# Last row pair of the first MLP product: P5 with hi and lo weights in one tile, its upper half copied after the hi part, the gelu table loaded earlier, one operand job later

## The chip, the cores and the metric

The kernel runs on one core of one Trainium2 chip. The metric is the device time of one execution in microseconds (us). A core has a matrix engine (TensorE, PE in the profile, with its weight loads as PEld), VectorE (DVE), ScalarE (ACT), GpSimd (POOL), which here does little more than issue the transfers that add to memory, and SyncE (SP), which issues the plain transfers.

## The reference

The input x has 2048 tokens of 640 channels. With xn the layer norm of x, the result is

```python
return x + _A_ref(xn, ...) + _B_ref(xn, B_w1, B_b1, B_w2, B_b2)
# A: a = xn @ hid_re.T, b = xn @ hid_im.T ; y = seq_re @ a - seq_im @ b   (real part of a 2D DFT)
# B: h = layernorm(xn); u = gelu(h.T @ w1 + b1); y = (u @ w2 + b2).T      (MLP across the tokens)
```

w1 is 2048 x 1728 and w2 1728 x 2048. 1728 is 13 blocks of 128 and a rest of 64, the "tail".

## The kernel before, in words

**Precision.** Every operand in float32 is split in two: a "hi" part, rounded to the matrix engine's fast float format by a ScalarE copy (`high`, L138), and a "lo" part, the rest, by a VectorE subtraction (`low`, L141). A product is three matmuls (`three`, L149, L150, L152): hi weights by hi data, hi weights by lo data, lo weights by hi data. When the lo weights are None, the third is left out.

**Seven products.** All big products are done in 2 x 2 blocks with seven products P1 to P7 in place of eight (a Strassen-like scheme). A unit is one pair of output row blocks, and its seven steps run in the order P1, P5, P6, P2, P7, P3, P4 (`row_steps`). The four output blocks C11, C12, C21, C22 are (row, half) = (0,0), (0,1), (1,0), (1,1); a half is 320 of the 640 channels. Sums of the weight blocks are made on VectorE: `first_sum` (L785) makes s = A21 + A22, others (L144) follow. A step's products run over 4 (or 5) blocks of 128 in the contraction, so 12 (or 15) matmuls of 320 columns.

**Stages.** First the sequence DFT (matmuls of 512 columns, until 405 us), then the hidden DFT (8 units, "hid"), then the first MLP product in two halves of the contraction (`up`, stage 0 and 1, 7 units each), then the second MLP product (`down`, twice 8 units). In `up`, unit r makes the row blocks r and r + 7 of the 1728 rows. Stage 0 stores its result to DRAM (`part_up[r]`, L907); stage 1 fetches that and adds it (L911, a POOL transfer), applies the gelu on ScalarE (L916), and so on.

**The last unit, r = 6, is special** (`tail`): its second row block has only 64 real rows. For P7 and P4, which use that block alone, the weight tile of 128 columns holds the hi part in the first 64 and the lo part in the other 64 (`cut_piece` with tail), so that two matmuls do the work of three, 8 per step instead of 12. The upper 64 rows of such a result are the lo weights' share. They are copied by ScalarE into a buffer (`by_dram`, L945), and a POOL transfer adds them to `part_up[6]` in DRAM (`add_to`, L934, 64 x 320). In stage 0 these adds are kept in the list `halves` and issued behind the store of the unit (`end`). In stage 1 the buffers of `by_dram` serve in every unit, for P2 and P7 (L941, 128 x 320): they are four quarters of one buffer, chosen by r and the product. P7 of unit 0 takes the quarter that P7 of the tail unit of stage 0 had.

**Where P5's result goes before.** P5 and P3 share a bank: P5's read copies it to C22, P3 then accumulates on top, and P3's read adds both to C12. P6 accumulates on P1's bank; P6's read copies to C12 and, in the tail unit, adds to C22 (L858, VectorE) and copies to C21 (L859, ScalarE).

**Order of the work.** Nothing is scheduled by a program; the order is written by hand (`turn_of`). Turn i issues, on the in-order queues: the loads of that turn, the read of the result of step i - 1, the sums, the hi part for step i + 2, the `extras`, the `timed` ones, a job, the lo part for step i + 2, and the matmuls of step i. So whatever waits on ScalarE or VectorE in a turn holds up the hi or lo part behind it. A "job" prepares the moving operand of a later stage. Long jobs (the tuples) only run in the turns that `LONG_AT` allows, as a pattern (positions, period) for each stage; the first pair is for hid. Another turn takes a job only if the next one is short.

Of the kernel before, what the change touches and what calls it, by code (L numbers as in the profile page):

```python
# [11 lines left out]
AF = mybir.ActivationFunctionType  # L12
ALU = mybir.AluOpType

P = 128
# [6 lines left out]
TAIL = F - NF * P  # L22
# [39 lines left out]


LONG_AT = (
    ((0, 1, 3, 6), 7), ((0, 1, 3, 6, 7, 8, 10, 14, 15, 17, 20), 21), ((0, 1, 3, 6), 7), ((0, 1, 3), 7),
)


# [1 line left out]
def fnet_plus_mixer(  # L70
# [99 lines left out]
    def cut_piece(source, n, tail=False, stacked=False):  # L170

        held = {}

        def of_tail():
            hi, src = (t.rearrange("p (q c) -> p q c", c=P) for t in (held["piece"][:, 0, :n], source()))
            return hi[:, :, :TAIL], hi[:, :, P - TAIL :], src[:, :, :TAIL]

        def top():  # L180
            cut_turn[0] = (cut_turn[0] + 1) % (AHEAD + 1)
            held["piece"] = keep.tile([P, 2, D], R32, name="piece", tag=f"cut{cut_turn[0]}")
            if tail:
                hi, _, src = of_tail()
                high(hi, src)
            else:
                high(held["piece"][:, 0, :n], source())

        def bottom():
            if tail:  # L190
                hi, lo, src = of_tail()
                low(lo, src, hi)
                return held["piece"][:, 0, :n], None
            hi, lo = (held["piece"][:, i, :n] for i in range(2))
            if stacked:
                last = slice(n - P, n)
                low(hi[TAIL:, last], source()[TAIL:, last], hi[TAIL:, last])
            whole = n - P if stacked else n
            low(lo[:, :whole], source()[:, :whole], hi[:, :whole])
            return hi, lo  # L200

        return top, bottom
# [564 lines left out]
    def row_steps(stage, nq, load_piece, at, end, bias=(None, None), base=None, earliest=0, each=None, aside={}, tail=False, stacked=()):  # L767

        s0, n = len(steps), nq * P
        raw, banks, held = {}, {}, {}

        def load(*names):
            for name in names:
                raw[name] = raw_slot(n)
                load_piece(raw[name], int(name[1]) - 1, int(name[2]) - 1)  # L780

        def first_sum():
            k = n if n == D else CH
            raw["s"] = raws[k][:, raws[k].shape[1] - 1, :n]
            nc.vector.tensor_add(raw["s"], raw["A21"], raw["A22"])  # L785
            if stacked:

                at = slice(n - P, n)
                nc.vector.tensor_copy(raw["s"][TAIL:, at], raw["A21"][TAIL:, at])

        order = (1, 5, 6, 2, 7, 3, 4)

        early = n < D
        loads_of = {-6: ("A11", "A21", "A22"), -4: ("A12",)} if early else {
            -5: ("A11",), -4: ("A21", "A22"), -1: ("A12",),
        }
        operand = {1: "A11", 5: "s", 6: "A11", 2: "A12", 7: "A21", 3: "A12", 4: "A22"}

        sums_of = {
            -2: (first_sum, lambda: sub(raw["A21"], raw["A11"], raw["A21"])),  # L800
            -1: (lambda: sub(raw["A11"], raw["s"], raw["A11"]),),
            2: (lambda: sub(raw["A12"], raw["A12"], raw["A11"]),),
        }
        bank_of = {1: "z", 6: "z", 7: "z", 4: "z", 5: "y", 3: "y", 2: "w"}
        new_bank = (1, 5, 2)
        if tail:
            bank_of.update({7: "v", 4: "v"})
            new_bank += (7,)
        of_moving = {1: 0, 2: 1, 3: 2, 5: 3, 7: 4, 4: 5, 6: 6}

        goes_to = {1: (0, 0, True), 5: (1, 1, True), 6: (0, 1, True), 2: (0, 0, False), 7: (1, 1, False),
                   3: (0, 1, False), 4: (1, 0, True)}

        def products(i):
            def run(w):
                if i in new_bank:
                    banks[bank_of[i]] = bank()
                for q in range(nq):
                    ks = slice(q * P, (q + 1) * P)
                    m = moving[stage, q]  # L820
                    three(
                        banks[bank_of[i]][:, :H2],
                        (w[0][:, ks], None if w[1] is None or i in stacked and q == nq - 1 else w[1][:, ks]),
                        (m[:, 0, of_moving[i], :], m[:, 1, of_moving[i], :]), i in new_bank and q == 0, q == nq - 1,
                    )
            return run

        def read(i):
            def run():
                if i == 1:  # L830
                    held["c"] = place[at]()
                row, half, fresh = goes_to[i]
                cols = slice(half * H2, (half + 1) * H2)
                c, b = held["c"][:, row, cols], banks[bank_of[i]][:, :H2]
                if tail and i in (7, 4):
                    nc.vector.tensor_add(c[:TAIL], b[:TAIL], c[:TAIL])
                    aside[i](row, half, b)
                elif i in aside:
                    aside[i](row, half, b)
                elif not fresh:  # L840
                    nc.vector.tensor_add(c, b, c)
                elif base and i == 4:

                    for k, queue in enumerate((nc.sync, nc.scalar)):
                        of = slice(k * H2 // 2, (k + 1) * H2 // 2)
                        nc.vector.tensor_add(c[:, of], b[:, of], base()[:, row, cols][:, of])
                        each(c, row, half, True, of, queue)
                    return
                elif base:
                    nc.vector.tensor_add(c, b, base()[:, row, cols])  # L850
                elif bias[row] is not None:
                    nc.scalar.activation(c, b, AF.Identity, bias=bias[row])  # L852
                else:
                    nc.scalar.activation(c, b, AF.Copy)  # L854
                if tail and i == 6:

                    low_row = held["c"][:, 1, :]
                    nc.vector.tensor_add(low_row[:, H2:], b, low_row[:, H2:])  # L858
                    nc.scalar.activation(low_row[:, :H2], b, AF.Copy)  # L859
                if each:  # L860
                    each(c, row, half, i in (2, 7, 3, 4))
                elif i == 4:
                    end(held["c"])
            return run

        for e, names in loads_of.items():
            loads[max(s0 + e, earliest)].append(lambda names=names: load(*names))
        if s0 == s_hid:


            operand[6] = "s"
            behind_lo[s0 - 2].append(first_sum)
            sums_of = {
                0: (lambda: sub(raw["s"], raw["s"], raw["A11"]),),
                1: (lambda: sub(raw["A21"], raw["A11"], raw["A21"]),),
                2: (lambda: sub(raw["A12"], raw["A12"], raw["s"]),),
            }
        for e, fs in sums_of.items():
            sums[s0 + e].extend(fs)
        for e, i in enumerate(order):  # L880
            steps.append(cut_piece(lambda i=i: raw[operand[i]], n, tail and i in (7, 4), i in stacked) + (products(i),))
            reads[s0 + e + 1].append(read(i))
        return s0

# [13 lines left out]
    def up(stage, r, at):  # L898
# [34 lines left out]
        def add_to(t, rows, row, half):  # L933
            nc.gpsimd.dma_start(part_up[r][rows, row, half * H2 : (half + 1) * H2], t, accum_op=ALU.add)  # L934

        def by_dram(i):
            def run(row, half, b):

                t = place["x1"]()[:, (r + (i == 4)) % 2, i // 7 * H2 : (i // 7 + 1) * H2]
                if not (tail and i in (7, 4)):  # L940
                    nc.scalar.activation(t, b, AF.Copy)  # L941
                    add_to(t, slice(P), row, half)
                    return
                t = t[P - TAIL :]
                nc.scalar.activation(t, b[P - TAIL :], AF.Copy)  # L945
                if stage == 0:
                    halves.append((row, half, t))
                else:
                    add_to(t, slice(TAIL), row, half)
            return run  # L950

        aside = (2, 7) if stage else ()
        if tail:
            aside += (7, 4)
        s0 = row_steps(
            f"up{stage}", 4, load_piece, at, end, earliest=s_up - 4, aside={i: by_dram(i) for i in aside}, tail=tail,
        )
# [65 lines left out]
    for r in range(NF2):  # L1023
# [4 lines left out]
        [gets[1]] + rests[0] + [gets[2]] + changes[1] + rests[1] + [gets[3]] + changes[2] + rests[2]  # L1028
        + changes[3] + rests[3]
    ))  # L1030
    for r in range(NF2):
        up(1, r, ("x2", "ca", "cb", "v", "x0")[r % 5])
    s_down = len(steps)
# [99 lines left out]
```

## Time and profile before

| | us |
|---|---|
| median of 3 runs (lowest, highest) | 876.68 (876.0, 876.92) |
| the profiled execution, whole | 875.92 |
| its span (first to last instruction) | 874.2 |
| mean granted TensorE clock | 0.999 |
| TensorE busy | 869.0 (99%) |
| VectorE / ScalarE / GpSimd busy | 711.7 / 530.2 / 126.2 |

A row of a timeline has the start, the duration, the engine, the line, the operation and what it writes and reads; in brackets stands how long the engine had been idle before it, and what ended that. [...] In a list of transfers the last number is the time from issue to landing. Times in a timeline count from the start of the span.

### The profile page before, as it was taken

The page shows a single profiled execution, that of the slowest core. Times are in us where ns is not written, and L with a number is a line of the kernel's source. Part 1 is how long each engine was busy: PE and PEld are TensorE (multiplying, and loading weights), DVE is VectorE, ACT ScalarE, POOL GpSimd, SP SyncE. Part 2 cuts the span into 40 slices and gives each one's busy share as a digit, 9 for nine tenths or more (in the row PEclk, how much of TensorE's full clock was granted, in tenths as well). Part 3 has the DMA queues.
Part 4 walks back from the last instruction along what each step waited for, and adds up shares of the span by engine and source line. Part 5 has one row for each costly group of instructions (what it writes and reads, how often), then busy time and mean ns, then how long its engine had stood idle before and what let it go on. Part 6 is the DMA issues. An engine that isn't in the chain of part 4 may idle for free.

```text
span 874.2 us, 13999 instructions
## 1 busy us (share of the span) xinstructions
PE 869.0 (99%) x4924; PEld 793.1 (91%) x4924; DVE 711.7 (81%) x1217; ACT 530.2 (61%) x960; POOL 126.2 (14%) x170
## 2 busy tenths in 40 slices
PE   9999999999999999999999999999999999999998
PEld 6888888888888888889999999999999999999998
DVE  7878878795887978788887787998678978897887
ACT  5746576764556566557565556675577766555553
POOL 0110100101121111222010101000212221111211
PEclk9999999999999999999999999999999999999999
DMA  7771554619385556869666756454678797766786
GB/s 270 231 266 76 194 203 132 242 59 357 54 219 92 163 119 133 208 92 195 168 127 166 156 139 196 162 177 138 142 170 181 169 244 193 190 136 133 151 173 139
DMA packets 86087, 147.64 MB, mean 169 GB/s; under 512 B 8512, under 2 KB 35904, under 8 KB 85760
## 3 DMA queue, kind: packets, MB, share of 16 engines
q1 hardware_dynamic: 64928, 95.80, 34.0%
q0 software_dynamic: 20800, 50.70, 30.6%
q8 instruction: 38, 0.62, 0.3%
q14 instruction: 33, 0.27, 0.1%
q10 hardware_dynamic: 288, 0.25, 0.1%
HBM read 99.96 MB, written 52.00 MB: 174 GB/s over the span
## 4 chain that ended last, share of the span: by engine, by line
PE 94%; DVE 3%; ACT 1%; DMA 1%; issue 1%; DVEq 0%; ACTq 0%
PE psum L149 30%; PE psum L150 30%; PE psum L152 29%; PE psum L477 5%; DVE piece L141 1%; DMA pieces<-y 1%; DVE pieces L144 0%; DMA x<-in_x 0%; ACT piece L138 0%; ACT n L259 0%; ACT x L259 0%; DVE pair L144 0%; DVE st L210 0%; DVE pieces L785 0%; DVE shid L141 0%
## 5 line engine op out<-in xcount | busy, mean ns | idle before, releaser
L141 DVE TENSOR_TENSOR piece<-pieces,piece 128x512 fp32r<-128x512 f32 (+2 forms) x524 | 350.1, 671 | 125.8 <-ACT piece L138 119.1
L138 ACT ACTIVATE piece<-pieces 128x512 fp32r<-128x512 f32 (+3 forms) x508 | 318.1, 627 | 212.0 <-PE psum L152 143.5
L150 PE MATMUL psum<-piece,n 128*128 128x512 f32 x504 | 196.4, 390 | 0.0
L149 PE MATMUL psum<-piece,n 128*128 128x512 f32 x504 | 196.2, 389 | 0.0
L152 PE MATMUL psum<-piece,n 128*128 128x512 f32 x504 | 196.1, 389 | 0.0
L149 PE MATMUL psum<-sup,piece 128*128 128x320 f32 x392 | 121.2, 310 | 0.0
L149 PE MATMUL psum<-sdown,piece 128*128 128x320 f32 x392 | 121.0, 309 | 0.0
L150 PE MATMUL psum<-sup,piece 128*128 128x320 f32 x392 | 120.9, 309 | 0.0
L150 PE MATMUL psum<-sdown,piece 128*128 128x320 f32 x392 | 120.9, 309 | 0.0
L152 PE MATMUL psum<-sup,piece 128*128 128x320 f32 x376 | 116.6, 310 | 0.0
L152 PE MATMUL psum<-sdown,piece 128*128 128x320 f32 x376 | 116.2, 309 | 0.0
L144 DVE TENSOR_TENSOR pieces<-pieces 128x512 f32<-128x512 f32 (+3 forms) x142 | 112.7, 794 | 2.6
L150 PEld LDWEIGHTS psum<-piece,n 128*128 128x128 f32 x504 | 94.6, 188 | 21.0 <-DVE piece L141 1.5
L149 PEld LDWEIGHTS psum<-piece,n 128*128 128x128 f32 x504 | 94.6, 188 | 19.9
L152 PEld LDWEIGHTS psum<-piece,n 128*128 128x128 f32 x504 | 94.6, 188 | 19.3
L152 PE MATMUL psum<-shid,piece 128*128 128x320 f32 x280 | 86.6, 309 | 0.1
L150 PE MATMUL psum<-shid,piece 128*128 128x320 f32 x280 | 86.5, 309 | 0.0
L149 PE MATMUL psum<-shid,piece 128*128 128x320 f32 x280 | 86.5, 309 | 0.0
L854 ACT ACTIVATE pair<-psum 128x320 f32<-128x320 f32 x102 | 44.5, 436 | 54.6 <-PE psum L152 49.8
L149 PEld LDWEIGHTS psum<-sup,piece 128*128 128x128 f32 x392 | 73.6, 188 | 0.6 <-ACT pairs L854 0.3
L149 PEld LDWEIGHTS psum<-sdown,piece 128*128 128x128 f32 x392 | 73.6, 188 | 0.2 <-ACT pair L852 0.2
L150 PEld LDWEIGHTS psum<-sup,piece 128*128 128x128 f32 x392 | 73.6, 188 | 0.0
(106 smaller groups left out, 1115.8 us busy)
## 6 DMA issues: line engine op xcount, KB each, us to landing
pieces<-in_dft_seq SPq DMA_DIRECT2D x128, 256.0 KB, 5.4
pieces<-in_w SPq DMA_DIRECT2D x88, 256.0 KB, 3.7
y<-c POOLq DMA_DIRECT2D x84, 256.0 KB, 6.1
out<-pair POOLq DMA_DIRECT2D x38, 320.0 KB, 5.3
pieces<-y SPq DMA_DIRECT2D x32, 320.0 KB, 3.9
pieces<-in_w SPq DMA_DIRECT2D x32, 192.0 KB, 3.1
out<-in_x SPq DMA_DIRECT2D x16, 320.0 KB, 7.1
up<-pair POOLq DMA_DIRECT2D x8, 640.0 KB, 3.2
```

Source lines behind the costliest of these rows:

```text
L138: nc.scalar.activation(hi, src, AF.Copy)
L141: nc.vector.tensor_sub(lo, src, hi.bitcast(F32))
L144: nc.vector.tensor_sub(to, a, b)
L149: nc.tensor.matmul(psum, wh, mh, start=first, stop=False, skip_group_check=True)
L150: nc.tensor.matmul(psum, wh, ml, start=False, stop=last and wl is None, skip_group_check=True)
L152: nc.tensor.matmul(psum, wl, mh, start=False, stop=last, skip_group_check=True)
L477: nc.tensor.matmul(banks[m, j], channels(k, j)[rows], w[cols], start=n == 0 and k == begin, stop=n == 2 and k == end, skip_group_check=True,)
L854: nc.scalar.activation(c, b, AF.Copy)
```

## The change

It has four parts.

1. In the tail unit P5 is treated like P7 and P4, in both stages of `up`. `first_sum` adds only the 64 real columns of each block of 128 and sets the others to zero (a VectorE memset). P5's hi and lo weights stand in one tile, so its step has 8 matmuls instead of 12. P5 gets a bank of its own ("u"), and P3 starts a fresh one. P5's read copies all 128 rows to C22; P6's read gets one more VectorE add (64 x 320), which adds P5's lower half to C12. P5's upper half is copied aside (64 x 320) and added in DRAM to both C12 and C22: two more POOL transfers in each stage, ahead of those of P7 and P4.
2. The copies aside of P5, P7 and P4 (`upper`) are issued in `extras` of the same turn, which is behind the hi part instead of ahead of it. The end of the unit follows the copy of P4.
3. A gelu of one element is issued in turn 7 of stage 1, which loads the gelu table there. Before, the table was loaded ahead of the first real gelu, in turn 14.
4. In hid, turn 6 no longer takes a long job. By the order of the changed program the jobs of the first operand run one slot later up to turn 24, and from turn 25 all is as before. In SP's queue the two loads of x for the second operand come after one more load of y.

```diff
 LONG_AT = (
-    ((0, 1, 3, 6), 7), ((0, 1, 3, 6, 7, 8, 10, 14, 15, 17, 20), 21), ((0, 1, 3, 6), 7), ((0, 1, 3), 7),
+    (tuple(i for i in range(56) if i % 7 in (0, 1, 3, 6) and i != 6), 56),
+    ((0, 1, 3, 6, 7, 8, 10, 14, 15, 17, 20), 21), ((0, 1, 3, 6), 7), ((0, 1, 3), 7),
 )
...
             raw["s"] = raws[k][:, raws[k].shape[1] - 1, :n]
+            if tail:
+                s1, a21, a22 = (raw[a].rearrange("p (q c) -> p q c", c=P) for a in ("s", "A21", "A22"))
+                nc.vector.tensor_add(s1[:, :, :TAIL], a21[:, :, :TAIL], a22[:, :, :TAIL])
+                nc.vector.memset(s1[:, :, TAIL:], 0.0)
+                return
...
         if tail:
-            bank_of.update({7: "v", 4: "v"})
-            new_bank += (7,)
+            bank_of.update({5: "u", 7: "v", 4: "v"})
+            new_bank += (7, 3)
...
-                if tail and i in (7, 4):
-                    nc.vector.tensor_add(c[:TAIL], b[:TAIL], c[:TAIL])
-                    aside[i](row, half, b)
-                elif i in aside:
+                if tail and i in (5, 7, 4):
+
+                    def upper():
+                        aside[i](row, half, b)
+                        if i == 4:
+                            end(held["c"])
+
+                    extras[s0 + order.index(i) + 1].append(upper)
+                    if i == 5:
+                        nc.scalar.activation(c, b, AF.Copy)
+                    else:
+                        nc.vector.tensor_add(c[:TAIL], b[:TAIL], c[:TAIL])
+                    return
+                if i in aside:
...
                     low_row = held["c"][:, 1, :]
+                    nc.vector.tensor_add(c[:TAIL], c[:TAIL], low_row[:TAIL, H2:])
                     nc.vector.tensor_add(low_row[:, H2:], b, low_row[:, H2:])
...
-            steps.append(cut_piece(lambda i=i: raw[operand[i]], n, tail and i in (7, 4), i in stacked) + (products(i),))
+            steps.append(cut_piece(lambda i=i: raw[operand[i]], n, tail and i in (5, 7, 4), i in stacked) + (products(i),))
...
-                t = place["x1"]()[:, (r + (i == 4)) % 2, i // 7 * H2 : (i // 7 + 1) * H2]
-                if not (tail and i in (7, 4)):
+                at = i in (5, 7)
+                t = place["x1"]()[:, (r + (i in (5, 4))) % 2, at * H2 : (at + 1) * H2]
+                if not (tail and i in (5, 7, 4)):
...
-                if stage == 0:
-                    halves.append((row, half, t))
-                else:
-                    add_to(t, slice(TAIL), row, half)
+                for k in (0, 1) if i == 5 else (row,):
+                    if stage == 0:
+                        halves.append((k, half, t))
+                    else:
+                        add_to(t, slice(TAIL), k, half)
...
+    extras[len(steps) + 7].append(lambda: nc.scalar.activation(one, one, AF.Gelu_apprx_tanh))
     for r in range(NF2):
         up(1, r, ("x2", "ca", "cb", "v", "x0")[r % 5])
```

More of the change, by code (lines that the diff above doesn't have):

```diff
@@ L953, in up @@
         if tail:
-            aside += (7, 4)
+            aside += (5, 7, 4)
         s0 = row_steps(
```

## The prediction

> **What bounds the kernel now.** I read the page first, then the chain of work that ended last, then the waits of the weight loads, then the timelines of single stretches.
>
> ```profile
> span 874.2 us, 13999 instructions
> PE 869.0 (99%) x4924; PEld 793.1 (91%) x4924; DVE 711.7 (81%) x1217; ACT 530.2 (61%) x960; POOL 126.2 (14%) x170
> PE 94%; DVE 3%; ACT 1%; DMA 1%; issue 1%; DVEq 0%; ACTq 0%
> 600.00:606.00 6.00, 6.00 (x43) 1.00 0.40 147
> 599.79 0.31 PE L150 MATMUL psum<-sup,piece 128*128 128x320 f32 x1
> 605.95 0.31 PE L150 MATMUL psum<-sup,piece 128*128 128x320 f32 x1
> ```
>
> TensorE is the path. The last three rows are a stretch of the first MLP product and its first and last matmul: 43 matmuls start within 605.95 - 599.79 = 6.16, so one costs 6.16/42 = 0.1467 us, not the 0.31 us it lasts. A whole step (12 matmuls) is 1.76 us, a step without lo weights (8) is 1.17. All that can be gained beside fewer matmuls is in the few places where TensorE stands. These are the ones near the change:
>
> ```profile
> 423.48 0.19 PEld L152 LDWEIGHTS psum<-shid,piece 128*128 128x128 f32 x1 [0.34 <-DVE piece L141]
> 618.00 0.19 PEld L149 LDWEIGHTS psum<-sup,piece 128*128 128x128 f32 x1 [0.28 <-ACT pairs L854]
> 642.98 0.19 PEld L149 LDWEIGHTS psum<-sup,piece 128*128 128x128 f32 x1 [0.26 <-ACT pair L854]
> 703.64 0.19 PEld L149 LDWEIGHTS psum<-sdown,piece 128*128 128x128 f32 x1 [0.19 <-ACT pair L852]
> ```
>
> Together 1.07 us. The profiled execution took 875.92 us, 0.76 below the median of the runs, 876.68. The sum is made against 875.92 and the difference is put on the median. 0.2% (1.75 us) is about what a measurement of this kernel can tell from no change.
>
> **Part 1: the matmuls.** P5 of the last row pair loses its third matmul: 4 in each of two stages, 8 in all, 8 x 0.1467 = -1.17 us, if nothing stands in the shorter step.
>
> **Part 2: the moved job.** Step 6 of the hidden stage no longer runs a long job.
>
> ```profile
> 421.35 0.49 DVE L141 TENSOR_TENSOR sup<-pair,sup 128x320 fp32r<-128x320 f32 x1
> 421.87 0.83 DVE L144 TENSOR_TENSOR pair<-pair 128x640 f32<-128x640 f32 x1
> 422.61 0.82 DVE L141 TENSOR_TENSOR piece<-pieces,piece 128x640 fp32r<-128x640 f32 x1
> 433.97 0.82 DVE L785 TENSOR_TENSOR pieces<-pieces 128x640 f32<-128x640 f32 x1 [1.20 <-DMA pieces<-y]
> ```
>
> The first two rows are that job; they hold up the third, for which TensorE stood until 423.48. Without them the piece starts at about 421.35, and the 0.34 us go: -0.34. The next jobs each move one slot. The job's last part (0.82 us on VectorE) now falls into the step after the 433.97 row, where VectorE was late through a load; it could cost up to 0.2 us. But the two x loads that ran beside that load now come after a later one in SP's queue, so it lands sooner. I take 0 (ends 0 and +0.2). The x loads keep three steps' distance to their reader. From the second x pair on (step 25) the order is the old one.
>
> **Part 3: the gelu table.**
>
> ```profile
> 640.48 1.28 ACT L916 ACT_TABLE_LOAD   x1
> 641.78 0.83 ACT L916 ACTIVATE pairs<-pairs,b_sb 128x640 f32<-128x640 f32 x1
> 642.51 0.42 ACT L854 ACTIVATE pair<-psum 128x320 f32<-128x320 f32 x1
> 628.95 0.44 ACT L854 ACTIVATE pair<-psum 128x320 f32<-128x320 f32 x1 [0.80 <-PE psum L152]
> ```
>
> Load plus gelu delay the P1 copy (third row) that the stand at 642.98 waits for: 0.26 us. The new place is just ahead of the fourth row, where ScalarE idled 0.80; the load's 1.28 makes that copy about 0.6 late, and its reader (P6) is one step away. So -0.26 (ends -0.26 and 0).
>
> **Part 4: the tail of the first half, up to P3.** In the P6 read a VectorE add (64x320) now stands between the two that were there. The chain before:
>
> ```profile
> 609.11 0.49 DVE L858 TENSOR_TENSOR pair<-psum,pair 128x320 f32<-128x320 f32 x1 [1.03 <-ACT pair L854]
> 609.64 0.44 ACT L859 ACTIVATE pair<-psum 128x320 f32<-128x320 f32 x1 [0.56 <-DVE pair L858]
> 609.97 0.93 ACT L138 ACTIVATE piece<-pieces 128x512 fp32r<-128x512 f32 x2
> 610.63 0.69 DVE L141 TENSOR_TENSOR piece<-pieces,piece 128x512 fp32r<-128x512 f32 x1 [1.02 <-ACT piece L138]
> 611.67 0.31 PE L152 MATMUL psum<-sup,piece 128*128 128x320 f32 x1
> 615.89 0.48 DVE L836 TENSOR_TENSOR pair<-psum,pair 64x320 f32<-64x320 f32 x1
> ```
>
> P3's lo was ready at 611.32; I estimate its weight load as due 0.10 ahead of the 611.67 matmul, so with 0.05 for the signal 0.2 was to spare. The new add costs 0.40 (a 64x320 add lasts 0.48, the next starts 0.40 after it). TensorE stands 0.2 and, as after the other stands, another 0.1 at the next load: of the 0.59 gained 0.30 stays. Behind that VectorE works without a pause, so it is only 0.2 earlier than before at the last row (P4's read). The boundary stand at 618.00 (0.28) came from ScalarE waiting for that read before it made the next hi part. The copies now come behind the hi part, so it goes. P5's read also gets a 64x320 copy on ScalarE (0.43), hidden beside P6. Its lo and hi parts shrink to 128x256, and first_sum is split into a narrower add and a memset of like sum. Together -0.57 (ends -0.86 and -0.2).
>
> **Part 5: the adds to DRAM, which decide.** P5's upper half goes to two places, so two 64x320 adds are put ahead of P7's and P4's in POOL's queue. The second of the two and P7's have the same destination; the changed program's P7 add waits for that one's landing. The P7 copy of the next row pair's first unit writes the buffer that P7's add reads, and waits for *its* landing. Before:
>
> ```profile
> 616.89 0.53 POOL L907 DMA_DIRECT2D up<-pair  x1 [12.27 <-ACT pairs L945]
> 620.63 1.73 POOL L934 DMA_DIRECT2D up<-pairs  x2 [3.20 <-ACT pairs L854]
> 624.64 0.44 ACT L941 ACTIVATE pairs<-psum 128x320 f32<-128x320 f32 x1 [1.86 <-DMA up<-pairs]
> 624.97 1.14 ACT L138 ACTIVATE piece<-pieces 128x512 fp32r<-128x512 f32 x2
> 625.63 0.69 DVE L141 TENSOR_TENSOR piece<-pieces,piece 128x512 fp32r<-128x512 f32 x1 [0.80 <-ACT piece L138]
> 626.99 0.31 PE L149 MATMUL psum<-sup,piece 128*128 128x320 f32 x1
> up<-pair POOLq DMA_DIRECT2D x1, 640.0 KB, 3.2
> up<-pairs POOLq DMA_DIRECT2D x2, 80.0 KB, 3.9
> up<-pairs POOLq DMA_DIRECT2D x1, 160.0 KB, 5.1
> ```
>
> Already before, ScalarE stood 1.86 us on P7's add, the first of the two at 620.63; queued behind that copy is the hi part (624.97) for the step that begins at 626.99. Now, in the times of before: the big store goes out 0.2 earlier, 616.68, and lands (3.2) at 619.9. The first add starts 0.5 later as it did, at 620.4, the second 0.6 behind it (the 1.73 of both allows at most 0.87), at 621.0, and lands (3.9) at 624.9. P7's add starts 0.5 after that, at 625.4, and lands at 629.3. The copy runs from 629.4 to 629.8, the hi part to 630.35, so the step starts at 630.4. Without the wait it would start at 626.99 - 0.57 = 626.42. TensorE stands 3.97 us; then the lo part, which normally is ready in time, comes 0.44 behind the third matmul's turn (0.69 and a signal after the hi part, against 2 x 0.1467), and 0.1 as above: +4.51. POOL's fetch for the first gelu goes out about 4 us later as well, but the gelu (641.78 before) moves by the same stand: hidden. Ends: both landings 3.2 give 3.1, both 5.1 give 6.9. I take the 3.9 of the same size and place.
>
> [...]
>
> **Part 6: the tail of the second half.** The same add, but ScalarE is full here (gelu, a job).
>
> ```profile
> 693.21 0.82 ACT L916 ACTIVATE pairs<-pairs,b_sb 128x640 f32<-128x640 f32 x1
> 694.56 0.43 ACT L854 ACTIVATE pair<-psum 128x320 f32<-128x320 f32 x1
> 695.02 0.49 DVE L858 TENSOR_TENSOR pair<-psum,pair 128x320 f32<-128x320 f32 x1
> 696.54 1.06 DVE L141 TENSOR_TENSOR piece<-pieces,piece 128x512 fp32r<-128x512 f32 x2 [0.29 <-ACT piece L138]
> 697.36 0.34 PE L152 MATMUL psum<-sup,piece 128*128 128x320 f32 x1
> ```
>
> P3's lo was already just late (the last row lasts 0.34, not 0.31). ScalarE does not get ahead with the 0.59: P5's extra copy (0.33 net of overlap) moves the 694.56 copy to about 694.7, the new add moves what follows by 0.40 more, so the lo part ends 0.56 later than before, at 697.8, where the shorter P5 wants it at 696.7. TensorE stands about 1.2; the P5 gain and more is lost: +0.56. The stand at 703.64 then goes (-0.19). Net +0.37 (ends -0.6 and +0.7).
>
> **Sum.** -0.34 - 0.26 - 0.57 + 4.51 + 0.37 = +3.71 (the -1.17 is inside parts 4 and 6): 879.63 against 875.92, 880.4 against the median.
>
> **Rivals.** *The wait is hidden after all (not slower).* Place: P7's add. With little else on the DMA engines while TensorE stands it may land quickly. What speaks against it: the copy waited 1.86 us with one add less ahead of it. Each us saved on the two landings is one us less; the point is a landing at about 627.3, where the stand is 2.55 and the change within 0.2%. Fully hidden it gives 876.68 - 0.80 = 875.9 (the sum without its 4.51).
>
> *TensorE loses its clock in the stand.* The only rows at a lower rate are the first ones:
>
> ```profile
> 1.24 5.14 PE L135 MATMUL psum<-idle 128*128 128x512 bf16 x12 [1.24 <-DVE idle L132]
> 39.75 20.56 PE L477 MATMUL psum<-piece,n 128*128 128x512 f32 x90
> ```
>
> 0.43 us each against 0.23 for the same width; such a phase cost 12 x 0.2 = 2.4 us. Once more after the stand: 882.8. The trace has no stand of some us in mid-kernel, so it neither shows nor excludes it. [...]
>
> *Slow adds.* Both land as slowly as the 160 KB one (5.1), because the adds read and write one region in turn: 880.4 + 2 x 1.2 = 882.8. The 80 KB row speaks against it.
>
> *The change saves what it may* (all of the 1.17, and the stands of 1.07): 874.4. Parts 4 to 6 speak against it.
>
> **How the numbers follow.** Forecast 0.55 (own range 879.0 to 881.6); clock lost 0.20; slow adds 0.10; wait mostly hidden 0.13 (875.9 to 878.4); all saved 0.02. The range is 878.0 to 883.0: its low end lets the hidden case out, its high end takes in the lost clock. Slower by over 0.2%: the first three and a little of the fourth, 0.86; within 0.2%: 0.11; faster: 0.03.
>
> **What would show it.** In the changed profile: a wait of some 6 us of ScalarE on the adds in the first unit of the second half, and one stand of TensorE of about 4 us beside it; no stand near 423, at the half's boundary or at the first gelu; stands of 0.2 to 0.3 at P3 of the first tail and about 1.2 at P3 of the second; matmuls 0.1467 apart after the long stand (0.25 or more would be the lost clock). The forecast is wrong if P7's add lands before 627, or if the copy doesn't wait for it.

## The result, and the profile after

The changed kernel takes 880.49 us (median of 6 runs, 878.75 to 881.03), the kernel before, beside it, 876.31 us (6 runs, 875.54 to 876.92). The ratio is 1.0045 with a 95% interval of 1.0035 to 1.0055: slower, by some 4 us. The six runs form two groups: two at 878.75 and 878.85 us with a mean granted clock of 0.999 and 1.000, and four from 880.35 us up with 0.997 or 0.998. The profiled one is of the first group, so the clock comes later, in the experiments.

From the page of the changed kernel: its span, the busy times, and the group of matmuls that waits most:

```profile
span 877.0 us, 13994 instructions
PE 867.3 (99%) x4916; PEld 791.9 (90%) x4916; DVE 711.6 (81%) x1221; ACT 531.0 (61%) x963; POOL 129.5 (15%) x174
L150 PE MATMUL psum<-sup,piece 128*128 128x320 f32 x392 | 121.2, 310 | 3.9 <-ACT pairs L959 3.0
```

TensorE has the 8 matmuls less, and the span is 2.8 us longer. The last row says where: TensorE stood 3.9 us ahead of hi matmuls of `up`, 3.0 of it for the ScalarE copy L959 (L941 before). These are the stands (times in which TensorE waits) in the changed part, from the waits of the weight loads:

```profile
610.79 0.19 PEld L153 LDWEIGHTS psum<-sup,piece 128*128 128x128 f32 x1 [0.32 <-DVE piece L142]
627.35 0.19 PEld L150 LDWEIGHTS psum<-sup,piece 128*128 128x128 f32 x1 [3.24 <-ACT pairs L959]
699.57 0.19 PEld L150 LDWEIGHTS psum<-sup,piece 128*128 128x128 f32 x1 [1.23 <-ACT piece L139]
700.29 0.19 PEld L153 LDWEIGHTS psum<-sup,piece 128*128 128x128 f32 x1 [0.43 <-DVE piece L142]
```

None of the four old ones (423.48, 618.00, 642.98, 703.64) is left. In their place there is one of 0.32 us at P3 of the first tail, one of 3.24 us in the first unit of the second half, and a pair at P3 of the second tail. ScalarE and GpSimd around the long one (timelines), and the transfers between 612 and 627 us (issues; the last number is us from issue to landing):

```profile
626.86 0.44 ACT L959 ACTIVATE pairs<-psum 128x320 f32<-128x320 f32 x1 [5.01 <-DMA up<-pairs]
627.20 1.14 ACT L139 ACTIVATE piece<-pieces 128x512 fp32r<-128x512 f32 x2
630.39 1.28 ACT L1052 ACT_TABLE_LOAD   x1
```
```profile
616.31 0.53 POOL L924 DMA_DIRECT2D up<-pair  x1 [12.19 <-ACT pairs L963]
619.83 1.72 POOL L951 DMA_DIRECT2D up<-pairs  x2 [2.98 <-DMA up<-pair]
624.13 2.58 POOL L951 DMA_DIRECT2D up<-pairs  x3 [2.58 <-issue]
```
```profile
up<-pair POOLq DMA_DIRECT2D x1, 640.0 KB, 3.2
up<-pairs POOLq DMA_DIRECT2D x4, 80.0 KB, 3.1
```

The chain is the one that was forecast: the store, then P5's two adds (the row of two at 619.83), then at 624.13 P7's add, which has waited for the second landing, then ScalarE, which stood 5.01 us until P7's add had landed. Two things differ. The adds land in 3.1 us, and P7's already at 626.8. (The gelu table is loaded at 630.39, the new place.) And TensorE stands for the copy itself, not for the hi part behind it. Its rows:

```profile
624.07 0.31 PE L153 MATMUL psum<-sup,piece 128*128 128x320 f32 x1
627.35 0.41 PE L150 MATMUL psum<-sup,piece 128*128 128x320 f32 x1 [2.98 <-ACT pairs L959]
```

The matmul at 627.35 is the first of P4, one step ahead of the one that the prediction had looked at. P4 accumulates on the bank that P7 used, so it cannot start until ScalarE has read P7's result out of that bank. A matmul's row lasts 0.31 us here and the next one starts 0.147 us after it; the distance of these two starts, 3.28 instead of 0.147, is a loss of 3.14 us.

The second tail's P3 (timelines of ScalarE and VectorE of the changed kernel):

```profile
694.66 0.41 ACT L139 ACTIVATE piece<-pieces 128x256 fp32r<-128x256 f32 x1
695.10 0.43 ACT L963 ACTIVATE pairs<-psum 64x320 f32<-64x320 f32 x1
695.56 0.83 ACT L933 ACTIVATE pairs<-pairs,b_sb 128x640 f32<-128x640 f32 x1
697.04 0.44 ACT L870 ACTIVATE pair<-psum 128x320 f32<-128x320 f32 x1
698.56 0.44 ACT L876 ACTIVATE pair<-psum 128x320 f32<-128x320 f32 x1 [1.08 <-DVE pair L875]
698.89 0.62 ACT L139 ACTIVATE piece<-pieces 128x512 fp32r<-128x512 f32 x1
```
```profile
697.51 0.48 DVE L874 TENSOR_TENSOR pair<-pair 64x320 f32<-64x320 f32 x1 [0.92 <-ACT pair L870]
698.03 0.49 DVE L875 TENSOR_TENSOR pair<-psum,pair 128x320 f32<-128x320 f32 x1
699.55 1.06 DVE L142 TENSOR_TENSOR piece<-pieces,piece 128x512 fp32r<-128x512 f32 x2 [0.29 <-ACT piece L139]
```

Ahead of P3's hi part (698.89) two new operations stand in series: P5's upper copy (L963, 695.10), and the add L874, on which L875 and so the copy L876 wait.

### The profile page after: what moved, and what is told of

The parts are those of the page before. It is cut to its first block, busy times and chain, and to the rows that moved or that the text cites. A ratio compares the mean times of both kernels' runs of the same rounds, so it can differ in the third digit from the quotient of the medians.

```text
span 877.0 us, 13994 instructions
## 1 busy us (share of the span) xinstructions
PE 867.3 (99%) x4916; PEld 791.9 (90%) x4916; DVE 711.6 (81%) x1221; ACT 531.0 (61%) x963; POOL 129.5 (15%) x174
```

## The experiments

Each run has the kernel before beside it on the same chip: 875.93 us in the first group (again, p7_first, p5_twice, small; 21 runs), 876.1 in the second (p7_second, tail_fix, c12_late, first_half_only; 25 runs), 875.91 in the third (fill_18, fill_4, again_2; 11 runs).

The theory: the loss is the chain store, P5's two adds, P7's add, copy; and the second tail's stands come from the two operations in front of its hi part. The rivals: the clock, which a stand that long may bring down; and a cost in other parts of the change (the moved job, the gelu table, the split itself).

**The change again.** No edit.

> The changed kernel unchanged, for its spread. Its six runs lie in two groups, 878.8 (two, granted clock 0.999 and 1.000) and 880.4 to 881.0 (four, clock 0.997 and 0.998), while the six runs of the kernel before lie within 875.5 to 876.9. Theory A (TensorE loses its clock after the stand of 3.2 us in some executions): again two groups about 1.9 us apart, the longer one with the lower clock, and in a profile of that group matmuls 0.25 us or more apart for some us after the stand, and nowhere else. Theory B (the landings of the two adds vary by 2 us): two groups, but the matmuls after the stand 0.147 apart and the stand itself longer by 1.9. Theory C (chance): one broad group around 880, clock and time not related.

> The changed kernel as it is, beside the two on the same chip: 880.5 to 881 us in most runs, and 878.8 us in those that keep the clock.

again: 881.03 us (5 runs, 880.71 to 881.55), ratio 1.0058 (1.0045 to 1.0071); again_2: 880.17 us (5 runs, 879.9 to 880.65), ratio 1.0049 (1.0037 to 1.0062). All ten have a mean clock of 0.996 to 0.998; with the first six, 14 of 16 runs are of the slower group. Both profiles are of that group. Stretches of the run again, and of again_2 (columns: the stretch, its length, busy us and count of PE, PEld, DVE, ACT and POOL, then the granted clock, the DMA share and GB/s):

```profile
624.78:628.09 3.31, 0.32 (x4) 0.05 (x2) 0.00 (x0) 0.49 (x2) 2.58 (x3) 1.00 0.93 184
628.09:629.10 1.01, 1.01 (x7) 1.01 (x8) 0.51 (x1) 0.98 (x2) 0.77 (x1) 1.00 0.85 117
629.10:632.50 3.40, 3.40 (x15) 3.40 (x14) 2.41 (x5) 1.60 (x3) 0.32 (x2) 0.50 0.52 62
632.50:640.00 7.50, 7.50 (x52) 7.50 (x52) 3.10 (x6) 4.69 (x10) 1.15 (x2) 1.00 0.70 158
```
```profile
624.00:627.24 3.24, 0.35 (x4) 0.09 (x2) 0.00 (x0) 0.49 (x2) 2.52 (x3) 1.00 0.92 197
627.24:630.70 3.46, 3.46 (x14) 3.46 (x15) 2.29 (x4) 1.02 (x3) 0.85 (x1) 0.53 0.79 91
630.70:640.00 9.30, 9.30 (x64) 9.30 (x64) 4.51 (x7) 6.50 (x14) 1.71 (x2) 0.99 0.56 130
```

Behind the stand the clock is half for about 3.4 us in both traces: 13 matmuls there start 0.267 us apart instead of 0.147, which is 13 x 0.12 = 1.56 us. In the run again it falls a full 1.0 us after work has resumed, so it isn't the resuming matmuls that are slow. The stand itself is as long as in the first profile (waits of the weight load of 3.26 and 3.15 us against 3.24), so slower landings are not the cause.

**The stand filled with work.** Two kernels with extra matmuls in the stand, whose result is not read. fill_18 is shown; fill_4 has 4 in place of 18.

```diff
+                if stage == "up1" and i == 4 and at == "x2" and not tail and s0 == s_up + 7 * NF2:
+                    for _ in range(18):
+                        nc.tensor.matmul(
+                            psum[(bank_turn[0] + 1) % 8][:, :H2], w[0][:, :P], moving[stage, 0][:, 0, 0, :],
+                            start=True, stop=True, skip_group_check=True,
+                        )
                 for q in range(nq):
```

> The changed kernel with 18 more matmuls of the same width (0.1467 us each, 2.64 us together) put ahead of the step that stands 3.24 us, into a bank that no one reads; they run in the stand. If the runs of 880.4 us and more are made by the clock, which idle time of TensorE in the stand brings down, the clock now stays full in every run, and all of them lie at 878.8 us or 1.6 to 2 us below the changed kernel beside it. If the second group of runs has another cause (slower landings, another stand), it is still there, with the same median as the changed kernel.

> The same with 4 such matmuls (0.59 us), which leaves about 2.6 us of idle time in one piece. If the clock falls only when a whole window of 3.41 us is idle, every run is at 878.8 us. If some 2.2 us of idle in one window are enough, as the profiles of the repeated and the doubled run suggest, about half of the runs (windows of 3.41 us against 2.6 us of idle: (0.8 + 2 x 0.4) / 3.41 = 0.47) lose it and lie 1.6 us or more above the others.

With 18: 878.62 us (7 runs, 878.09 to 878.74), ratio 1.0031 (1.0020 to 1.0042), every clock 0.999 or 1.000. The slower group is gone, 1.55 us below again_2 on the same chip, close to the 1.56 us of the profile (the adds land 0.1 us sooner than in again_2, so the match is good to about that). With 4: 880.23 us (5 runs), ratio 1.0044 (1.0031 to 1.0056): 878.54 and 879.32 with clock 1.000, three from 880.23 to 880.61 with 0.997 or 0.998. TensorE's timelines of the two, of fill_18 first:

```profile
623.97 2.80 PE L826 MATMUL psum<-sup,piece 128*128 128x320 f32 x18
626.99 0.41 PE L150 MATMUL psum<-sup,piece 128*128 128x320 f32 x1 [0.22 <-ACT pairs L965]
```
```profile
624.33 0.75 PE L826 MATMUL psum<-sup,piece 128*128 128x320 f32 x4
627.93 0.42 PE L150 MATMUL psum<-sup,piece 128*128 128x320 f32 x1 [2.84 <-ACT pairs L965]
```

So in these runs the clock goes with the idle time: with a stand of 0.22 us in the profile all seven runs of fill_18 keep it, with one of 2.84 us three of the five of fill_4 lose it. fill_4 left more idle time than planned, 2.84 us, because in its profile the adds landed later (in 3.4 us); three of five is about half, as the second branch of its expectation had it. The windows of 3.41 us in that expectation are the pieces of 3.413 us that the last section counts in the traces, and its 2.2 us are an estimate from 2.38 and 2.33 us of idle time in such a piece in the traces of again and p5_twice. The expectation of p7_second, below, takes the same two numbers. No trace has between 1.8 and 2.3 us there, so the 2.2 us are not shown as a limit. How the single executions differ is read from the traces in the last section.

**P7's add first, and P7's add second.** The order of the four adds alone; the indices 0 to 3 are P5 to C12, P5 to C22, P7 and P4. p7_first, then p7_second:

```diff
-                for row, half, t in halves:
+                for row, half, t in [halves[k] for k in (2, 0, 1, 3)] if halves else ():
```
```diff
-                for row, half, t in halves:
+                for row, half, t in [halves[k] for k in (0, 2, 1, 3)] if halves else ():
```

> Only the order of the four adds to DRAM behind the first half is changed: P7's goes first, P5's two behind it. The theory that the stand of 3.24 us comes from P7's add standing third, behind a landing: the stand shrinks to the 0.1 of the kernel before, the time to 875.6 (878.75 less 3.2 in the faster group), one group of runs, since nothing is long enough to lose the clock. Rival, that the adds' traffic or the shorter step is to blame: 878 or more, the stand stays in another place.

> The changed kernel with the four adds of the first tail in the order P5 to C12, P7, P5 to C22, P4: P7's add is for another part of the result than the one before it and waits for no landing. If the 3.24 us stand at 627.35 is the chain of two landings (3.1 us each), it shrinks to 0.6 us or less, and with less than 2.2 us of idle in any 3.41 us the clock stays full: about 876 us in every run, beside 875.7 us with P7's add first. If instead any add ahead of P7's costs the path its own landing, about 3 us of stand stay, and the clock is lost in most runs: 879 us or more.

p7_first: 875.74 us (11 runs, 875.3 to 876.19), ratio 0.9998 (0.9989 to 1.0006). p7_second: 875.9 us (10 runs, 875.6 to 876.51), ratio 0.9997 (0.9988 to 1.0006). Every clock is 0.999 or 1.000. ScalarE's copy, in p7_first and in p7_second:

```profile
623.14 0.44 ACT L959 ACTIVATE pairs<-psum 128x320 f32<-128x320 f32 x1 [1.49 <-DMA up<-pairs]
```
```profile
624.06 0.44 ACT L959 ACTIVATE pairs<-psum 128x320 f32<-128x320 f32 x1 [1.97 <-DMA up<-pairs]
```

The wait falls from 5.01 to 1.49 and 1.97 us, and TensorE's stand of 3.24 us is gone (0.2 us remain at that place in p7_second). One add ahead of P7's costs no more than these 0.2 us, as long as P7's doesn't wait for its landing. All that the adds cost in the first half comes from the one pair of adds to the same part of the result.

**P5's add twice.** P5's share of C22 is added twice, so that the output is another one by that share; it makes one more landing in the chain.

```diff
-                for row, half, t in halves:
+                for row, half, t in [halves[k] for k in (0, 1, 1, 2, 3)] if halves else ():
```

> The add of P5's upper half to C22 is issued twice behind the first half (the result holds that small share twice), so that P7's add waits for one more landing. The chain theory: the stand grows by one landing and one start, 3.1 + 0.5 = 3.6 us, to about 6.8. [...] Theory B: two groups or a broad one, from 882.4 up, clock 0.999.

884.08 us (4 runs), ratio 1.0091 (1.0077 to 1.0105), against 881.03 for the change beside it. The stand in TensorE's timeline, and stretches around it:

```profile
630.74 0.64 PE L150 MATMUL psum<-sup,piece 128*128 128x320 f32 x1 [6.08 <-ACT pairs L959]
```
```profile
624.00:627.00 3.00, 0.67 (x5) 0.40 (x3) 0.19 (x1) 0.00 (x0) 0.81 (x1) 1.00 0.77 196
627.00:633.80 6.80, 3.06 (x11) 3.06 (x12) 2.30 (x4) 1.47 (x3) 3.44 (x4) 0.50 0.67 72
633.80:640.00 6.20, 6.20 (x43) 6.20 (x43) 2.68 (x4) 4.78 (x10) 0.88 (x1) 1.00 0.60 98
```

One landing more makes the stand 6.08 - 2.98 = 3.1 us longer, which is the landing time of the transfers, and the time 3.05 us longer (the expectation had added 0.5 us for the start of the add). The adds to one place ran one after the other here too; that is the chain. The clock here is half for 6.8 us, 3.7 us of it (627.00 to 630.74) within the stand; the mean clock of all four runs is 0.995 or 0.996.

**The job and the table alone.** The kernel before with the moved job and the early gelu only.

```diff
-    ((0, 1, 3, 6), 7), ((0, 1, 3, 6, 7, 8, 10, 14, 15, 17, 20), 21), ((0, 1, 3, 6), 7), ((0, 1, 3), 7),
+    (tuple(i for i in range(56) if i % 7 in (0, 1, 3, 6) and i != 6), 56),
+    ((0, 1, 3, 6, 7, 8, 10, 14, 15, 17, 20), 21), ((0, 1, 3, 6), 7), ((0, 1, 3), 7),
...
+    extras[len(steps) + 7].append(lambda: nc.scalar.activation(one, one, AF.Gelu_apprx_tanh))
```

> The kernel before with two parts of the change alone: the hidden stage's job one slot later, and the gelu table loaded early. Both stands (0.34 near 423 and 0.26 near 643) go and no other comes: 0.6 us less, about 875.7 against 876.3, within what a measurement can tell; the profile decides. Rival: a job's last part makes VectorE late near 438, a stand of up to 0.2 there.

875.19 us (10 runs, 875.07 to 875.28), ratio 0.9991 (0.9981 to 1.0). TensorE no longer stands near 423 and 643; the stand at the boundary of the halves stays (waits of the weight loads):

```profile
617.62 0.19 PEld L150 LDWEIGHTS psum<-sup,piece 128*128 128x128 f32 x1 [0.28 <-ACT pairs L855]
```

0.74 us below the kernel before on the same chip, against 0.60 forecast; the interval just reaches no difference, so the time alone would not show it, but the two stands are gone from the trace. And p7_first, which is this plus the split of P5 without the long chain, is 0.55 us above it: eight matmuls less, and still a loss.

**What the split costs in the second tail.** Three kernels, all with P7's add ahead of P5's. tail_fix moves the upper copy of P5 behind its own lower copy four steps later (which puts P7's add first by itself) and takes the lower rows of C12 from the finished row; c12_late does only the latter, on p7_first; first_half_only, on p7_first, leaves P5 of the second half as it was before.

```diff
-                    extras[s0 + order.index(i) + 1].append(upper)
+                    extras[s0 + (6 if i == 5 else order.index(i) + 1)].append(upper)
...
-                    nc.vector.tensor_add(c[:TAIL], c[:TAIL], low_row[:TAIL, H2:])
                     nc.vector.tensor_add(low_row[:, H2:], b, low_row[:, H2:])
                     nc.scalar.activation(low_row[:, :H2], b, AF.Copy)
+                    nc.vector.tensor_copy(c[:TAIL], low_row[:TAIL, H2:])
```

That is tail_fix; c12_late has its second part, and p7_first's order. first_half_only, wherever P5 is named as split:

```diff
+        cut = () if not tail else (5, 7, 4) if stage == "up0" else (7, 4)
...
-                if tail and i in (5, 7, 4):
+                if i in cut:
```

> The changed kernel with two moves: P5's upper copy four product steps later, behind its own lower copy (P7's add then goes out first), and the lower rows of C12 moved by one VectorE copy behind the low row's last add instead of an add ahead of it. If the second tail's stands (1.23 and 0.43 us, at 699.57 and 700.29) come from P5's upper copy in front of the hi part on ScalarE and from the add of 0.54 us in front of the lo part on VectorE, they shrink to 0.5 us or less in sum, and the 3.24 us stand is gone: about 874.4 us, 1.3 us below 875.7 with P7's add first, and below the kernel before. If the order of the copies is not what delays the hi part, the second tail keeps 1.2 us or more, and the time is about 875.5 us.

> P7's add first, and only the VectorE move of the run before (the lower rows of C12 copied behind the low row's last add); P5's upper copy stays early. It splits the second tail's causes. If the add of 0.54 us delays both parts, the second tail's stands (1.13 and 0.33 us with P7's add first) lose about 0.5 us in the hi part and keep 0.6 us; if only the copies on ScalarE delay the hi part, its 1.1 us stays and only the lo part's 0.3 us goes. About 875.3 us or 875.6 us.

> P7's add first, and P5 split only in the first half; the second half's last row pair is as in the kernel before. The second tail then loses its 0.59 us of saved matmuls and its stands of 1.13 and 0.33 us with their 0.21 us of short waits, and gets back the kernel before's own short stand there. If the split costs more in the second half than it saves, this is 0.7 us or so faster than 875.7 us: about 875.0 us. If the stands there are only moved from a later step, it is slower: about 876.2 us.

tail_fix: 874.17 us (9 runs, 873.83 to 874.65), ratio 0.9979 (0.9969 to 0.9989). first_half_only: 874.54 us (10 runs, 874.42 to 875.43), ratio 0.9984 (0.9975 to 0.9993). c12_late: 874.62 us in its one run. The weight loads' waits at P3 of the second tail, in p7_first, in c12_late and in tail_fix:

```profile
696.12 0.19 PEld L150 LDWEIGHTS psum<-sup,piece 128*128 128x128 f32 x1 [1.23 <-ACT piece L139]
696.85 0.19 PEld L153 LDWEIGHTS psum<-sup,piece 128*128 128x128 f32 x1 [0.43 <-DVE piece L142]
```
```profile
695.46 0.19 PEld L150 LDWEIGHTS psum<-sup,piece 128*128 128x128 f32 x1 [0.71 <-ACT piece L139]
696.18 0.19 PEld L153 LDWEIGHTS psum<-sup,piece 128*128 128x128 f32 x1 [0.43 <-DVE piece L142]
```
```profile
695.72 0.19 PEld L153 LDWEIGHTS psum<-sup,piece 128*128 128x128 f32 x1 [0.41 <-DVE piece L142]
```

The add is worth 1.23 - 0.71 = 0.52 us of the hi part's stand, as the first branch of the expectation had it. The other 0.71 us goes with the copy on ScalarE, whose timeline in tail_fix at that place is this:

```profile
691.34 0.41 ACT L139 ACTIVATE piece<-pieces 128x256 fp32r<-128x256 f32 x1
691.65 0.83 ACT L933 ACTIVATE pairs<-pairs,b_sb 128x640 f32<-128x640 f32 x1
```

From the start of P7's hi part to the gelu it takes 0.31 us, and 0.90 (694.66 to 695.56) in the changed kernel: the copy costs 0.59. The lo part's 0.4 us stays in all three. In c12_late and tail_fix VectorE comes to the lo part without a pause from the last add, with an operation of a job (0.81 us) right ahead of it; and in first_half_only, where P5's step is not shortened, there is no stand at this P3. So VectorE did not get ahead with the 0.59 us; whether moving the job would help was not tried. Of the three expectations, c12_late's times were too high (875.3 and 875.6 against 874.62): the same edit also takes away the stand of P3 in the first tail (610.79 in the changed kernel), which they had left out. first_half_only ends below its 875.0: it sheds stands of 1.67 us for 0.59 us of matmuls, and the stand at the boundary, which the expectation had set against that, did not come back. tail_fix is the fastest of all, 1.9 us below the kernel before.

## Why the prediction was right, and where it was not

The direction and the place were right, and the median, 880.49 us, is almost the 880.4 us forecast; but that is two errors that cancel, and so in part luck. Without the loss of the clock the change takes 878.6 us (fill_18). The forecast was 1.8 us above that: 0.9 by the sum (3.71 against the 2.8 us between the spans) and 0.8 by the offset (below). The clock added 1.55.

| part | forecast, us | profile, us | from |
|---|---|---|---|
| 2, the moved job | -0.34 | -0.3 | stand at 423 gone |
| 3, the gelu table | -0.26 | -0.3 | stand at 643 gone |
| 4, first tail and boundary | -0.57 | -0.44 | -0.59, +0.43 at P3, -0.28 at 618 |
| 5, the adds to DRAM | +4.51 | +3.24 | 3.14, and 0.10 at the next load |
| 6, second tail and boundary | +0.37 | +0.89 | -0.59, +1.23, +0.44, -0.19 |
| sum | +3.71 | +3.1 | the spans differ by 2.8 |

The remaining 0.3 us lies in small differences over the span: 0.14 in the start-up, and 0.09 because P4's second matmul was late by that much before already (its rows are below).

**Parts 2 and 3** came out as worked out, and the run with these two alone has both stands gone. The doubt left in part 2 was a late load of y. In all twelve traces with the moved job VectorE's wait for y at 433.97 (1.20 us before) is gone. In five of them there is a wait for y near 448 in its place, and where it is longer than some 0.5 us it reaches TensorE: 0.99 us in the run again and 0.67 in fill_4, with stands of 0.49 and 0.17, against 0.16 to 0.51 us and no stand in again_2, fill_18 and tail_fix. The weight load's wait in the run again:

```profile
454.49 0.19 PEld L153 LDWEIGHTS psum<-shid,piece 128*128 128x128 f32 x1 [0.49 <-DVE piece L142]
```

That stand cost 0.5 us with the next load. The one trace of the kernel before has no wait near 448, so the moved loads probably bring it there; that is not shown.

**Part 4.** P3's stand of 0.2 and the 0.1 behind it are there; another 0.1 us came at a load after it. The 0.05 us that the forecast took for a signal is in the profile of before: the piece ends at 423.43 (422.61 + 0.82) and the weight load that waits for it starts at 423.48. The weight load of the 611.67 matmul started at 611.52, 0.15 us ahead of it, where the estimate had it due 0.10 ahead.

**Part 5, the deciding term, was mis-sized, in three steps.** First the landings: 3.9 us was taken from the median of two transfers of this size; 3.1 was measured, and P7's own add was there 2.7 us after its issue; why they land sooner than before isn't shown. The copy so began 2.1 us earlier than forecast (626.86 is about 627.3 in the times of before, against 629.4). Second, the chain to TensorE is shorter: P4 needs only the copy, not the hi part behind it, 0.5 us, and the 0.44 us of the lo part then fall away, being hidden behind P4. Third, P4 was due 1.76 us earlier than the step that was looked at. -2.1 - 0.5 + 1.76 = -0.8 us on the stand (3.97 to 3.14). The bank that P7 and P4 share was in the code. In the profile of before its wait hardly shows. P7's copy ended at 625.08 (624.64 + 0.44) and P4 began at 625.14, 0.147 us behind the matmul ahead of it, so on time; only its second matmul came 0.24 us after the first, the short delay that otherwise follows a stand (618.00 to 618.25 there):

```profile
625.14 0.40 PE L149 MATMUL psum<-sup,piece 128*128 128x320 f32 x1
625.38 0.30 PE L150 MATMUL psum<-sup,piece 128*128 128x320 f32 x1
```

One sign that the prediction had named for being wrong came about: in the profile's own times P7's add landed at 626.8, before 627 (about 627.3 in the times of before). By its working such a landing leaves a stand of 2.55 us; it was 3.24 with the next load, because P4 waited and not the step behind it.

**Part 6 was too small by 0.5 us.** The mechanism is shown by c12_late and tail_fix, but both operations cost more than priced: the add 0.52 us instead of 0.40 (697.51 to 698.03; L875 writes the row that this add reads, and starts only when it is done), and the copy 0.59 instead of 0.33. So the hi part too was late, where the forecast had only the lo part late.

**The offset.** The sum was put on the median of the three runs shown, 0.76 us above the profiled execution. The medians of the kernel before are 876.31 us beside the result (6 runs) and 875.91 to 876.1 beside the experiments (57 runs), close to the profiled 875.92: most of the 0.76 us was the scatter of three runs.

**The rivals.** "TensorE loses its clock in the stand" had 0.20; it happened in 14 of 16 runs, at 1.55 us and not at 2.4, since the half rate held for some 3.4 us only, 13 matmuls at 0.267 us each. "Wait is hidden" did not happen, but its idea that the landings are quicker was half right. "Slow adds" did not happen.

## What to carry to other kernels

When a program makes each of several accumulating transfers to one place wait for the one before, as here, they are a chain of whole landings, 3.1 us each in the changed kernel: put first the one whose buffer is needed first, or one that goes elsewhere between them; here that order alone was worth 5.3 us (881.03 against 875.74 on one chip), some 1.55 us of it the clock. A saving of 0.59 us of matmuls in one step is lost if its evictions gain two small operations in front of the next operand's hi part: price an operation by what it does to the starts of those behind it (0.52 and 0.59 us here for durations of 0.48 and 0.43), not by the overlap that it might have. And when looking for who waits for a late copy, look for the next user of the memory that it reads, not only for what is queued behind it.

## What the runs showed of the hardware that was not expected

A stand with 2.9 to 3.0 us of idle time (in the three traces of the changed kernel) went with a lower clock (a mean of 0.996 to 0.998) in 14 of its 16 executions. The traces' records of the granted clock say when it changes. In these five traces every stretch between two changes is a whole number of pieces of 3.413 us, which is how long the clock was half in again and again_2:

| run | stretches between changes, us | pieces |
|---|---|---|
| the kernel before | 866.99 full | 254 |
| the first profile of the change | 870.40 full | 255 |
| again | 624.64 full, 3.413 half, 245.76 full | 183, 1, 72 |
| again_2 | 621.23 full, 3.413 half, 249.17 full | 182, 1, 73 |
| p5_twice | 621.23 full, 6.827 half, 249.17 full | 182, 2, 73 |

This is TensorE's idle time in the pieces around the stand, counted in each trace from its first change. It is an estimate, good to some 0.15 us: it counts from the end of the last row, 0.31 us after that matmul's start, and a next matmul would have started after 0.147.

| run | piece, us | idle in it, us | then |
|---|---|---|---|
| again_2 | 624.06 to 627.47 | 2.89 | half |
| again | 625.70 to 629.12 | 2.38 | half |
| p5_twice | 623.58 to 627.00 | 2.33 | half |
| the first profile of the change | 622.79 to 626.20, and the next | 1.82, 1.15 | full |
| fill_4 | 623.20 to 626.61, and the next | 1.53, 1.32 | full |

In these five the clock was half behind a piece with 2.33 us of idle time or more, and stayed full behind pieces with 1.82 us or less. The stand is nearly the same in again_2 (2.89 us, all in one piece) and in the first profile (2.98 us, in two pieces): what differs is where it lies among the pieces of that execution. Where between 1.8 and 2.3 us the limit lies, or whether there is one, these few traces do not say.

In p5_twice one more accumulating transfer of 80 KB to the same place, which the program makes wait for the one before, cost one full landing, 3.1 us. In p7_second one that goes to another place, ahead of P7's, cost the path at most the 0.2 us of stand that p7_second has there and p7_first has not.
